# A fused attention and gated FFN kernel: the first batch's values computed token-major, the exchanged halves made by TensorE, the first FFN column finished first, later loads moved

**Chip, cores, metric.** One core of a Trainium2 chip. The metric is the device time of one execution in microseconds (us), smaller is better. An execution's time is about 1.7 us more than the span that its trace shows. "Order of time" means the list of an engine's instructions by their start; "the chain" is the chain of waits, followed back from the last instruction to what released each step.

## The reference, cut to what matters

```python
# q, k, v: (8 batches, 8 heads, 576 tokens, 64);  f: (8, 8, 576)
cum    = cumsum(log(clip(f, 1e-4, 1)))
scores = q @ k.T / 8 + cum[:, :, :, None] - cum[:, :, None, :]     # causal
x      = (softmax(scores) @ v) -> (4608 tokens, 512)
out    = (sigmoid(x @ w_gate) * (x @ w_val)) @ w_out               # d_ff = 1536
```

The decay of a key is folded into the values (`vg` = v times a factor per key), so the kernel computes exp(scores) and two sums: over values, and over the factors alone (the softmax's denominator).

## The kernel before

Batch 0 has nothing to run beside: its attention is a prologue. After it the FFN of one batch and the attention of the next share TensorE. Heads go in pairs (four per batch). A "column" is 128 of the 1536 FFN columns, gate and value; its product takes 16 matmuls over eight slots of `xR`, four with the heads in their own half of the partitions and four with the halves exchanged. The scores of a pair come in three units; their exp tiles are eA, eB and eC in the traces (for pair 2 of the changed kernel they lie in gv), and GpSimd lays the causal mask on each.

```python
def S_unit(p, u, slot, tag=None):          # scores of one unit, exp, causal mask
    ...
    nc.scalar.activation(e[...], ps[...], ACTF.Exp, scale=scale)
    nc.gpsimd.affine_select(out=m, in_=m, ...)

def out_one(p, bs, bv):                    # batch 0, one pair of heads
    pair_region(p, 512 * bs, 0, MAIN, False)      # ten matmuls with constant weights: sums
    nc.vector.transpose(Z, ps[:, bs, :])          # sums, reciprocal, spread again
    inverse(r, Z)
    spread(R, r)
    yield
    pair_region(p, 512 * bv, 0, MAIN, True)       # ten matmuls: values, features in partitions
    scaled(p, 512 * bv, R, 0, MAIN)               # xR = values * R
    if p == 0:
        cross_x(p, 1, 0, MAIN)                    # exchanged halves by two DMAs

def swap(p, bank):                         # exchanged halves by a matmul with a swap matrix
    nc.tensor.matmul(ps[:, bank, :], swap_bf, xR[:, p, 0:MAIN], start=True, stop=True)
    nc.scalar.copy(xR[:, HPAIR + p, 0:MAIN], ps[:, bank, :])

# ... the start of the program: loads
load_v(0, 0, 4, range(NJT), nc.sync)
load_qk(0, 0, ((0, 2), (2, 4)))            # GpSimd issues q and k
load_qk(0, 1, ((0, 4),))
load_v(0, 4, 8, range(NJT), nc.gpsimd)
load_w1(0, 512)
# ... the end of the prologue: columns 0 and 1 interleaved with the last pair's steps
swap(1, 0)
g1_slots(0, 0, (0, 1), True, False)        # column 0, slots 0 and 1
burst = out_one(HPAIR - 1, 2, 3)
next(burst)
g1_slots(0, 1, (0, 1), True, False)        # column 1, slots 0 and 1
swap(2, 1)
next(burst, None)
g1_slots(0, 0, (2, 5), False, False)
S_unit(0, "Z", 0, "D")
g1_slots(0, 1, (2, 5), False, False)
g1_slots(0, 0, (4, 6), False, False)
swap(3, 2)
g1_slots(0, 1, (4, 6, 3), False, False)
g1_slots(0, 0, (3, 7), False, True)
g1_end(0, 0)
g1_slots(0, 1, (7,), False, True)
g1_end(0, 1)
```

The softmax here doesn't subtract the row's maximum and nothing guards it: scores larger than these inputs give would overflow.

## Time and profile before

| | before |
|---|---|
| time, median of 3 (range) | 374.73 us (374.28 to 375.12) |
| first transposes of q and k | 6.72 us |
| first exponential | 8.93 us |
| last exponential of batch 0 starts | 21.6 us |
| first matmul of FFN column 2 | 29.37 us in the order of time, 29.87 in the chain |

The last row is the mark to follow: from there on TensorE is nearly always busy, so what the prologue gains or loses shows as a shift of that matmul. The two readings differ because of how column 2 starts: its first matmul began at 29.37, its second, into another PSUM bank, only at 29.87, and there the chain takes it up.

TensorE at the border, in the order of time (start, length, engine, line, operation, out<-in, form, count):

```profile
28.61 0.83 PE L195 MATMUL ps<-ident_bf,qk_in 64*64 64x64 bf16 x72
29.37 1.97 PE L455 MATMUL ps<-xR,w 64*128 64x512 bf16 x13
```

The 72 transposes end at 28.61 + 0.83 = 29.44, so the 0.70 us that the chain puts down to VectorE (29.12 to 29.82, in the prediction's lines) lie mostly beside transposes. Only column 2's second matmul waits for it.

### The profile page before, as it was taken

The numbers are of one execution on the slowest core, as the hardware profiler recorded it, in microseconds if no ns is written. First come the engines' busy times: TensorE is split into PE (matmuls) and PEld (weight loads), VectorE is DVE, ScalarE is ACT, GpSimd is POOL, SyncE is SP. The second block draws the span as 40 slices with busy tenths as digits, with TensorE's granted clock in tenths as the row PEclk, the third lists the DMA queues.
The fourth block names the chain that finished last, engine by engine and source line by source line (L and its number), as shares of the span: only waits on it lengthen the run. The fifth ranks groups of instructions, "written<-read, shape, count | busy, mean of one in ns | idle before, by whom it ended". The sixth has DMA issues, their size and how long they took to land.

```text
span 373.4 us, 12210 instructions
## 1 busy us (share of the span) xinstructions
PE 359.3 (96%) x5259; PEld 192.0 (51%) x5264; DVE 176.5 (47%) x382; ACT 195.7 (52%) x294; POOL 168.3 (45%) x265
## 2 busy tenths in 40 slices
PE   2889999999999999999999999999999999999996
PEld 1547545455555545454665566545456544444442
DVE  5775482557375555274708370737064703312320
ACT  5868754574736472848374727471747313323321
POOL 8896745064826663559665946460415000000000
PEclk9999999999999999999999999999999999999999
DMA  8999999599988976789984996596313131011002
GB/s 157 233 209 256 194 182 217 173 213 154 158 164 196 157 84 63 168 182 134 142 185 105 185 177 138 148 159 83 99 59 76 32 102 58 3 56 58 0 24 90
DMA packets 101350, 49.24 MB, mean 132 GB/s; under 512 B 72001, under 2 KB 94401, under 8 KB 101297
## 3 DMA queue, kind: packets, MB, share of 16 engines
q0 software_dynamic: 48704, 20.65, 44.0%
q1 hardware_dynamic: 52448, 27.68, 30.8%
q8 instruction: 41, 0.67, 0.8%
q10 hardware_dynamic: 144, 0.13, 0.1%
q14 instruction: 13, 0.10, 0.1%
HBM read 37.90 MB, written 9.44 MB: 127 GB/s over the span
## 4 chain that ended last, share of the span: by engine, by line
PE 94%; ACT 2%; DMA 1%; issue 1%; DVE 1%; POOL 0%; ACTq 0%; POOLq 0%
PE ps L455 51%; PE ps L495 17%; PE ps L352 8%; PE ps L504 8%; PE ps L241 6%; PE ps L195 2%; PE ps L300 1%; DMA qk_in<-in_k_dram 1%; ACT eC L246 1%; ACT eB L246 0%; ACT eA L246 0%; ACT kT L200 0%; PE ps L417 0%; DVE kT L200 0%; POOL qk_in L97 0%
## 5 line engine op out<-in xcount | busy, mean ns | idle before, releaser
L455 PE MATMUL ps<-xR,w 64*128 64x512 bf16 x1728 | 205.1, 376 | 0.2
L465 DVE SCALAR_TENSOR_TENSOR gv<-sg,ps 128x512 bf16<-128x512 bf16 x108 | 74.0, 686 | 152.2 <-ACT sg L464 149.0
L455 PEld LDWEIGHTS <-w 64*128 64x128 bf16 x1728 | 86.2, 94 | 84.0 <-issue 2.5
L464 ACT ACTIVATE sg<-ps 128x512 bf16<-128x512 f32 x108 | 64.5, 598 | 85.1 <-PE ps L455 83.9
L248 POOL TENSOR_SCALAR_AFFINE_SELECT eC<-eC 128x256 bf16<-128x256 bf16 x32 | 12.9, 404 | 94.4 <-ACT eC L246 94.4
L241 PE MATMUL ps<-qT,kT 64*128 64x320 bf16 (+6 forms) x416 | 47.0, 275 | 2.0 <-ACT kT L200 1.1
L246 ACT ACTIVATE eC<-ps 128x896 bf16<-128x896 f32 (+1 forms) x32 | 28.1, 878 | 20.7 <-PE ps L241 20.4
L257 POOL TENSOR_TENSOR vg<-vb,g_bf 128x640 bf16<-128x640 f32 x30 | 37.8, 1261 | 0.0
L482 ACT ACTIVATE ob<-ps 128x512 f32<-128x512 f32 x35 | 19.6, 596 | 32.2 <-PE ps L504 20.1
L495 PE MATMUL ps<-wox,gvx 64*128 64x512 bf16 x288 | 35.7, 376 | 0.0
L241 PEld LDWEIGHTS <-kT 64*128 64x128 bf16 x416 | 22.9, 96 | 24.0 <-issue 4.9
L246 ACT ACTIVATE eA<-ps 128x896 bf16<-128x896 f32 (+2 forms) x33 | 30.5, 926 | 9.0 <-PE ps L241 8.5
L495 PE MATMUL ps<-wo,gv 64*128 64x512 bf16 x288 | 34.4, 376 | 0.0
L246 ACT ACTIVATE eB<-ps 128x768 bf16<-128x768 f32 (+2 forms) x33 | 27.4, 832 | 10.0 <-PE ps L241 9.2
L504 PE MATMUL ps<-wo,gv 128*128 128x512 bf16 x140 | 32.1, 380 | 0.3 <-issue 0.2
L271 DVE TENSOR_TENSOR xR<-ps,R 128x64 bf16<-128x64 f32 (+2 forms) x68 | 26.2, 429 | 2.1
L108 POOL DMA_DIRECT2D vb<-in_v_dram x30 | 25.2, 849 | 0.2 <-issue 0.2
L263 DVE STREAM_TRANSPOSE R<-r 128x576 f32<-128x576 f32 (+1 forms) x32 | 24.6, 770 | 1.1
L495 PEld LDWEIGHTS <-gvx 64*128 64x128 bf16 x288 | 15.7, 94 | 13.0 <-issue 0.4
L495 PEld LDWEIGHTS <-gv 64*128 64x128 bf16 x288 | 15.3, 94 | 13.7 <-issue 0.5
L246 ACT ACTIVATE eD<-ps 128x640 bf16<-128x640 f32 x30 | 21.1, 702 | 2.0 <-PE ps L241 2.0
L504 PEld LDWEIGHTS <-gv 128*128 128x128 bf16 x144 | 13.4, 98 | 16.7 <-issue 1.4
(82 smaller groups left out, 325.9 us busy)
## 6 DMA issues: line engine op xcount, KB each, us to landing
out_dram<-ob SPq DMA_DIRECT2D x35, 256.0 KB, 2.2
vb<-in_v_dram POOLq DMA_DIRECT2D x20, 256.0 KB, 5.4
xR<-xR SPq DMA_DIRECT2D x20, 144.0 KB, 4.1
gvx<-gv SPq DMA_DIRECT2D x12, 192.0 KB, 4.8
vb<-in_v_dram SPq DMA_DIRECT2D x8, 256.0 KB, 7.3
k_rows<-in_k_dram POOLq DMA_DIRECT2D x16, 128.0 KB, 6.0
q_rows<-in_q_dram POOLq DMA_DIRECT2D x16, 128.0 KB, 5.6
qk_in<-in_q_dram POOLq DMA_DIRECT2D x7, 288.0 KB, 6.7
```

The lines of the kernel that those rows point to most:

```text
L108: eng.dma_start(vbs[b % 2][0:n, t, h0:h1, :], rows)
L241: nc.tensor.matmul(ps[:, sc + h, c:c + i1 - i0], k_at(p, jt)[hp, :], qT[hp, i0:i1], start=True, stop=True)
L246: nc.scalar.activation(e[:, :, 0:w], ps[:, sc:sc + 2, 0:w], ACTF.Exp, scale=scale)
L257: (eng or nc.gpsimd).tensor_tensor(out=vg[:, :, :, 0:D], in0=vbs[b % 2][:, :, 2 * a:2 * a + 2, :], in1=g_bf[:, :, 2 * p:2 * p + 2].unsquee ...
L263: nc.vector.transpose(R.rearrange("p (n c) -> p n c", c=32), r.unsqueeze(2).to_broadcast([128, r.shape[1], 32]))
L271: nc.vector.tensor_tensor(out=xR[:, a, r0:r0 + n], in0=psf[:, o + i:o + i + n], in1=R[:, i:i + n], op=ALU.mult)
L352: nc.tensor.matmul(psf[32 * qd:32 * qd + 32, o + a:o + z], lhsT_of(jt, qd), e_of(u, qd)[:, c:c + z - a], start=(y == 0), stop=(y == len(to ...
L455: nc.tensor.matmul(ps[:, bk, :], w1[half, head, ft * NP:(ft + 1) * NP], xR[half, sl, t0:t0 + TCH], start=(first and x == 0), stop=(last an ...
L464: nc.scalar.activation(sg, ps[:, fb, :], ACTF.Tanh, scale=0.5)
L465: nc.vector.scalar_tensor_tensor(out=gv[:, ft, :], in0=sg, scalar=1.0, in1=ps[:, fb + 1, :], op0=ALU.add, op1=ALU.mult)
L495: nc.tensor.matmul(ps[:, bk, :], lhsT, rhs, start=(x == 0 and ft == 0), stop=(x == 1 and ft == NFT - 1))
L504: nc.tensor.matmul(ps[:, 4 + tt, :], gv[:, ft, tt * NP:(tt + 1) * NP], wo[:, ft, :], start=(ft == 0), stop=(ft == NFT - 1))
```

## The change

Its intent: spare the prologue work. Values are computed with tokens in the partitions (the exp tile is the stationary operand, `vg` with one more column the moving one), so the 65th column of each product is the sum and the constant-weight matmuls fall away. The normalised result is turned back by TensorE transposes, in both orders of the halves, so that pairs 1 to 3 need no swap matmul and no DMA. Values are loaded pair by pair and mostly after q and k. Column 0 is finished before column 1 starts. The output weights and the q/k of later batches load at later steps.

```diff
+    def vals_main(p, bank, todo):            # 40 matmuls of 65 columns for a pair
+        ...
+    def norm_main(p, bank):                  # reciprocal of column 65, product, into gv
+        ...
+    def back(p, its, swapped, at):           # turn back, own or exchanged halves
+        ...
-    load_v(0, 0, 4, range(NJT), nc.sync)
     load_qk(0, 0, ((0, 2), (2, 4)))
...
-    load_v(0, 4, 8, range(NJT), nc.gpsimd)
-    load_w1(0, 512)
...
+    load_v(0, 0, H, (NJT - 1,), nc.sync)
+    load_v_pair(0, 0)
+    load_qk(0, 1, ((0, 4),))
+    load_v_pair(0, 1)
...
     T_step(0, 4, ACTC, DVEC)
+    nc.scalar.activation(gT, cum, ACTF.Exp, ...)     # was before T_step
+    load_v(0, 4, 8, range(NJT - 1), nc.gpsimd)
+    S_unit(0, "U", 0)
...                                            # in the loop over pairs
+        if p == 0:
+            load_w1(0, 512)
+        main_unit(p, 2)                        # the scores, exp and mask of unit eC
...                                            # the end of the prologue
+    vals_main(3, 0, EARLY3)
+    norm_main(3, 0)
+    back(2, range(4), 0, main_at)
+    back(2, range(4), 1, lambda it: 2048 + NP * it)
+    nc.scalar.copy(xR[:, HPAIR + 2, 0:MAIN], psh[:, 2048:2048 + MAIN])
+    vals_main(3, 1, LATE3)
+    norm_main(3, 1)
+    nc.vector.tensor_copy(split(xR[:, 2, 0:MAIN]), main_of)
     g1_slots(0, 0, (0, 1), True, False)
...
+    for swapped, copy in ((0, nc.vector.tensor_copy), (1, nc.scalar.copy)):
+        o = 3072 + MAIN * swapped              # both halves in PSUM bank 3
+        back(3, range(4), swapped, lambda it: o + NP * it)
+        copy(xR[:, HPAIR * swapped + 3, 0:MAIN], psh[:, o:o + MAIN])
+    g1_slots(0, 0, (2, 5, 4, 6), False, False)
...
     g1_slots(0, 0, (3, 7), False, True)
     g1_end(0, 0)
+    S_unit(0, "Z", 0, "D")
+    g1_slots(0, 1, (0, 1, 2, 5, 4, 6, 3, 7), True, True)
     g1_end(0, 1)
...
-    for x, w in enumerate((5, 9, 12)):         # steps at which wo loads
+    for x, w in enumerate((5, 19, 20)):
-    for x, w in enumerate((18, 21, 22, 23)):   # steps at which later q/k load
+    for x, w in enumerate((21, 23, 50, 54)):
```

## The prediction

> **What bounds the kernel now.** I read the page first, then busy time by stretch, then the chain of waits over the first 64 us, then the order in time of GpSimd, VectorE and TensorE there, and last the DMA traffic of the first 9 us.
>
> The page gives the frame: engine totals, then TensorE by slices of 9.3 us.
>
> ```profile
> span 373.4 us, 12210 instructions
> PE 359.3 (96%) x5259; PEld 192.0 (51%) x5264; DVE 176.5 (47%) x382; ACT 195.7 (52%) x294; POOL 168.3 (45%) x265
> PE   2889999999999999999999999999999999999996
> ```
>
> TensorE is idle 14.1 us in all, and almost only in the first slices and in the last. The stretches say it in us (columns: stretch, length, busy time and count of PE, weight load, DVE, ACT, POOL, then clock, DMA share, GB/s):
>
> ```profile
> 0.00:17.08 17.08, 9.36 (x168) 5.71 (x172) 10.86 (x29) 11.03 (x14) 15.16 (x31) 1.00 1.00 194
> 17.08:28.61 11.53, 10.44 (x153) 5.48 (x154) 7.86 (x14) 7.64 (x12) 10.53 (x17) 1.00 1.23 209
> 28.61:62.00 33.39, 32.89 (x583) 18.45 (x582) 16.36 (x33) 24.39 (x38) 21.84 (x38) 1.00 1.15 211
> ```
>
> The change rewrites the prologue, all that comes before the repeating FFN steps. That border is at 28.61 us, where the 72 transposes of the next batch start. After it TensorE loses 0.5 us in 33, and its work there is not changed. So the time moves by about as much as the first matmul of FFN column 2 moves. In the chain that matmul starts at 29.87, 0.75 us after TensorE was free, because VectorE has not emptied column 0's banks:
>
> ```profile
> 28.68 0.43 PE ps L195 x36
> 29.11 0.01 issue
> 29.12 0.70 DVE gv L465
> 29.82 0.04 issue
> 29.87 2.77 PE ps L455 x23
> ```
>
> The start of the prologue hangs on loads. In the window 3 to 9 us the queue of q and k (q0) has to share with that of v (q1), and carried 0.66 MB in 6 us, 110 KB/us; alone it later runs at about 200 GB/s:
>
> ```profile
> q0 software_dynamic: 633, 0.66, 65.1%
> q1 hardware_dynamic: 2314, 0.57, 47.3%
> ```
>
> In the chain the first k piece is awaited until 6.68 (2.07 + 4.61). From 8.93 to 22.19 the exponentials and copies keep ScalarE busy for about 11.5 of 13.3 us.
>
> **What the Trainium skill says.** "TensorE: Matmul & The Clock Gate", Part 1: the array starts at half clock and is released after some 3.4 us of sustained work, judged in free-running windows. The trace agrees in effect: 36 transposes take 0.69 to 0.80 us up to 13 us and 0.50 at 17.00. The clock row does not show it. The same page, in its part on the 56 ns gap, puts the floor of start-to-start at about 25 ns; here 39 matmuls of 65 columns on half-width tiles stand in the chain with 0.81 us, 21 ns each, so I use the trace. "Trainium Kernel Development and Optimization", Key Constraints: the queues share the same 16 DMA engines; the two q lines above agree. "TensorEngine Tiling", PSUM Bottleneck: faster TensorE packing does not speed up emptying PSUM. That is the crux below.
>
> **The change, part by part.**
>
> *Removed on TensorE:* per pair of heads, the ten matmuls with the constant weights that make sums already spread over 64 rows (1.27 us cold at 13.29, 0.7 warm), the ten value matmuls (1.21 and 0.7), and the swap matmuls (3 x 0.39). *Added:* 40 value matmuls of 65 columns per pair, whose last column is the sum: 0.81 us warm, 1.25 cold (estimate from 0.81 and the half clock, as they are partly bound by issue); and 8 transposes back per pair (16 for pairs 1 to 3, own and swapped half): half of 16 x 128 columns at the rate of 512 columns in 0.21 us is 0.45 warm. So 2.5 cold becomes about 2.1, and 1.7 warm becomes about 1.3: 1 to 1.5 us less TensorE work, where TensorE waits anyway for much of the time.
>
> *VectorE:* per pair it loses a transpose of the sums (0.72), a spreading transpose (0.71) and keeps a reciprocal (0.25) and a product (0.69); it gains a copy back (0.65 for 512 columns, from 0.76 for 576) and, for pairs 2 and 3, the scaled values that GpSimd made in 1.26 (0.95 each on VectorE with its small copy). Four pairs: 9.5 + 1.9 = 11.4 before, (0.24 + 0.71 + 0.65 + 0.95) x 4 = 10.2 after. Hardly less, and in a chain.
>
> *Loads:* v comes by pair, after q and k, so q and k have the engines nearly alone from about 4.6 us. 288 KB then land at about 5.95 instead of 6.68: 0.75 us gained at the head.
>
> Now the chain, in the order of the new program's queues, with the durations of the old one. First transposes 5.95; copies 6.7 to 7.45; first scores 7.5; the exp of the decays now stands after the copy on ScalarE (7.35 to 8.1), so the first exp starts at 8.15 (before 8.93) and the exps of pair 1 at 11.75 (before 12.10).
>
> Then GpSimd. Its ten issues after the identity (v pair, q, k, v pair, four v) at 0.75 or 0.63 each run from 4.45 to 11.7. Masks of eA and eB follow to 12.75; then two issues of FFN weights (0.7 each) stand **before** the mask of eC, which ends at about 14.55 (before: 13.88). The values of pair 0 need it, and stand in TensorE's queue ahead of the scores of pair 2. So they end at about 15.5, scores of pair 2 at 16.15, its exp starts at 16.2 (before 16.75). Of the 0.75 gained, 0.55 is left.
>
> From 15.55 VectorE is the chain: normalise pair 0 (0.95) 16.5; values of pair 1 scaled 17.4; copy 18.1; q copy 18.85; normalise pair 1, after its values, 19.8; scaled 20.7; copy 21.35; scaled 22.25; normalise pair 2 at 23.15; first half of pair 3 23.8. TensorE then turns pair 2 back (0.5) and makes the late half of pair 3 (0.6): 24.3. Normalise 24.95; copy pair 2 25.6; copy pair 3 26.3. The product of column 0 with the slots that need them (12 matmuls, 107 ns each) ends at 26.95, the small Z scores at 27.15. All 16 of column 1 (1.73) come after: 28.9. Two sets of transposes: 29.3.
>
> There column 2 can start at once, as column 0's banks were emptied from 27.0 to 28.3. So 29.35 against 29.87: **0.5 us gained**: 0.75 from the bank wait that is gone, less 0.2 because the prologue itself ends no earlier. Moving the output weights and q/k loads changes no wait that I find: in the chain, wo is not awaited, and its loads now issue at about 47.5 us with the queue empty, some 10 us before use. I take 0.2 more for less crowding in the queue, and round to 373.9 from 374.73.
>
> **Rivals.**
> (a) *GpSimd or VectorE is quicker than I say.* The old first mask took 0.95 where its kind takes 0.40, next to a VectorE product; with less collision the chain starts 0.5 earlier, and shorter VectorE operations give 1 us more: 372.5. For it: the new form spares TensorE and GpSimd (two products of 1.26). Against: VectorE got that work.
> (b) *Late clock.* TensorE stands still for about 1.2 us at 13.3 to 14.5, before the values of pair 0. If the window that released the clock at 17.0 is thereby not full, the release comes one 3.4 us window later. I reckon 0.3 to 0.5 us, as VectorE paces that stretch: 374.3; more if TensorE turns out to pace it: 375.
> (c) *Loads of later stages shift the wait.* FFN weights 0 to 511 issue at 12.75 and land near 20, before column 0 at 24.3; but if the software queue is slower, column 0 waits. Or the later issues of wo and of q/k of batch 3 come too late: wo's last third issues at step 20 and is needed at step 32, q/k of batch 3 have 13 steps. Old landings take 2.5 us for 512 KB plus 1.7 to start. Unlikely; would cost 1 to 2 us: 375.5.
> (d) *Column-first order costs.* Column 1's 16 products cannot fill waits for pair 3 any more. In the old program they did; this is in my sum (1.73 after column 0), and is what eats most of the gain. If pair 3 is ready sooner than 26.3, it is a gain of up to 1.5.
>
> **Range and chances.** The border can move only inside the prologue: TensorE is busy 19.8 us of it (9.36 + 10.44), loses at most 1.5 of that, and cannot begin before about 6, so the border would stay past 24 even without idle time; a gain of 2% (7.5 us) needs it at 21. I give it 0.02, for what I cannot see. A loss of 7.5 us needs a new wait in every later stage: 0.01. (a) and (d) together reach 372.3, (b) and (c) 375.3; that is my range, near 8 in 10.
>
> **What would show it.** Right: first transposes of k near 6.0; first exp near 8.15; values of pair 0 held by the mask of eC until about 14.5; VectorE without gaps from 16 to 24; no wait on VectorE before column 2, which starts near 29.3. Wrong: column 2 before 28 (VectorE was not the chain) or after 30.5 (late clock or a load); any wait over 0.5 us on wo, FFN weights or q/k after 30 us.

## More of the kernel before

The waits of TensorE in the first 30 us of the kernel before (columns: who <- for whom: us in total, times, longest):

```profile
PE ps L195 <- DMA qk_in<-in_q_dram: 5.5, 1, 5.5
PE ps L241 <- ACT kT L200: 1.1, 1, 1.1
PE ps L195 <- DMA qk_in<-in_k_dram: 1.0, 1, 1.0
PE ps L300 <- DVE Z L319: 0.5, 1, 0.5
```

Only the first is long, and it is the first load.

At the end of the prologue the products of columns 0 and 1 (L455) stand between the other steps, and from the values of pair 3 on the chain names no wait (start, us, what):

```profile
24.67 0.74 PE ps L300 x10
25.41 0.54 PE ps L455 x4
25.95 0.15 PE ps L241 x10
26.09 0.86 PE ps L455 x8
26.95 0.32 PE ps L332
27.28 1.40 PE ps L455 x12
```

## The result, and the profile after

| | before | after |
|---|---|---|
| time, median of 4 (range) | 374.50 us (373.98 to 375.12) | 376.93 us (376.42 to 377.68) |
| span of the profiled execution | 373.4 | 374.7 |
| first transposes | 6.72 | 6.19 |
| first exponential | 8.93 | 8.40 |
| last exponential of batch 0 starts | 21.6 | 21.6 |
| column 2 in the order of time (in the chain) | 29.37 (29.87) | 30.64 (30.71) |
| second pair of matmuls of column 2 | 29.87 | 30.87 |
| first transposes to column 2, in the order of time | 22.65 | 24.45 |
| of it TensorE idle, in gaps over 60 ns | 2.34 | 4.58 |

The ratio of the times is 1.0066, with a 95% interval of 1.0042 to 1.0089: slower, by less than 2%. (Ratios here are the mean time of one kernel's fast runs over that of the other's of the same rounds, so not quite the ratio of the medians that I quote.) The predicted time was 373.9 and the range ended at 375.3, so the result is outside.

Taken as a sum, the rest of the kernel is level: from column 2 to the end, the trace of before has 373.4 - 29.37 = 344.03 us and that of after 374.7 - 30.64 = 344.06. So the net difference of the two traces, 1.3 us, is that of the prologue. In its parts the rest is not the same: after stops for 1.28 us at 109.13 (told below), and TensorE of before is busy 0.9 us less in 80 to 100, 120 to 140 and 240 to 260 us (19.76, 19.57 and 19.70 us, against 19.94, 20.00 and 20.00). The profiled execution of before was the slowest of its runs and that of after the quickest of its, which is why the medians differ by 2.4.

The page of after, to set against the first lines in the prediction:

```profile
span 374.7 us, 12464 instructions
PE 358.2 (96%) x5393; PEld 192.2 (51%) x5397; DVE 174.2 (46%) x384; ACT 195.4 (52%) x295; POOL 168.5 (45%) x262
```

TensorE's busy time fell by 1.1 us and yet the span rose by 1.3. So it waits more. Its waits in the first 31 us of after:

```profile
PE ps L202 <- DMA qk_in<-in_q_dram: 5.0, 1, 5.0
PE ps L202 <- DMA qk_in<-in_k_dram: 2.1, 2, 1.2
PE ps L248 <- DVE kT L207: 0.9, 1, 0.9
PE ps L248 <- DVE vg L265: 0.7, 1, 0.7
PE ps L375 <- DVE xR L664: 0.6, 1, 0.6
```

The first is shorter by half a microsecond: the head start. The second holds, with its longest of 1.2 us, k of heads 4 to 7, for which before did not wait. The third is the first scores waiting for the copied keys; before, the decay's transposes filled that stretch, and now they come after it. The last is new: TensorE waits for a copy by VectorE. The chain of waits of after, in two parts (start, us, what; pieces of "issue" under 0.05 us left out):

```profile
6.60 7.05 DMA qk_in<-in_k_dram
13.70 0.69 PE ps L202 x18
14.39 0.33 PE ps L248 x2
14.71 1.43 PE ps L347 x40
16.14 0.56 PE ps L248 x2
16.72 1.94 ACT gv L255 x2
...
20.17 1.32 POOL w L159 x2
21.49 1.09 POOL eA L257
22.58 0.61 POOL eB L257
23.23 0.32 PE ps L347 x8
...
25.79 0.43 DVE xR L664
26.27 0.41 PE ps L375 x8
26.68 1.40 PE ps L507 x12
28.08 0.14 PE ps L248 x10
28.23 1.73 PE ps L507 x16
29.95 0.76 PE ps L202 x72
30.71 1.83 PE ps L507 x16
```

The first part says that the second half of k, issued at 6.60, landed only 7.05 us later, and that the third set of transposes waited for it. In before it took about as long (7.3 us) but was issued at 5.23: what moved it is that the first values now stand ahead of it in GpSimd's queue. By 16.72, when the exponentials of pair 2 start, the head start is gone (16.75 before). Between the parts the chain runs over GpSimd: two issues of FFN weights and the masks of pair 3. The second part is the end: VectorE copies pair 3, only then do eight transposes make its exchanged half, only then 12 matmuls finish column 0, and column 1's 16 follow in one piece. Nothing is left to run beside those steps.

Where the 1.27 us between the two columns 2 arise can be read off the last exponential, which starts at 21.59 in before and at 21.65 in after: up to there 0.06 us are lost (the head start is gone), and 1.21 after it. That stretch repeats. It takes 7.78, 7.79, 7.78 and 8.12 us in before, `before_lateloads`, `before_warm` and `before_keep`, and 8.99, 9.15, 8.86, 8.85, 8.99 and 8.63 in after, `after_again`, `after_oldloads`, `after_warm`, `after_head` and `after_both`, which leave the end as the change has it. In all ten traces the full clock had been granted before that stretch began, so the clock does not make this part of the difference.

GpSimd at the two places where it holds masks back (in brackets: idle before, and what ended it):

```profile
13.94 0.69 POOL L159 DMA_DIRECT2D w<-in_moe_w_val_dram  x1 [0.43 <-DMA qk_in<-in_k_dram]
14.63 0.42 POOL L257 TENSOR_SCALAR_AFFINE_SELECT eC<-eC 128x256 bf16<-128x256 bf16 x1
...
21.48 1.09 POOL L257 TENSOR_SCALAR_AFFINE_SELECT eA<-eA 128x256 bf16<-128x256 bf16 x1
```

The issue at 13.94 waited for the landing of the k load that uses the same semaphore: GpSimd's loads signal on eight semaphores in turn (numbers 99 to 106 in the trace), so the ninth load waits until the first has landed. The mask at 21.48 took 1.09 us instead of about 0.40, beside a VectorE product of two operands in SBUF from 21.50 to 22.32. "GPSIMD Engine Reference", Specifications, of the Trainium skill names contention of GpSimd with such VectorE instructions; the trace agrees.

### The profile page after: what moved, and what is told of

Read it like the earlier page. It is cut to its first block, busy times and chain, and to the rows that moved or that the text cites. A ratio compares the mean times of both kernels' runs of the same rounds, so it can differ in the third digit from the quotient of the medians.

```text
span 374.7 us, 12464 instructions
## 1 busy us (share of the span) xinstructions
PE 358.2 (96%) x5393; PEld 192.2 (51%) x5397; DVE 174.2 (46%) x384; ACT 195.4 (52%) x295; POOL 168.5 (45%) x262
## 3 DMA queue, kind: packets, MB, share of 16 engines
q0 software_dynamic: 48864, 21.11, 45.8%
## 4 chain that ended last, share of the span: by engine, by line
PE 90%; ACT 2%; POOL 2%; DMA 2%; DVE 1%; issue 1%; POOLq 0%; ACTq 0%; DVEq 0%
PE ps L507 49%; PE ps L547 17%; PE ps L556 8%; PE ps L404 8%; PE ps L248 5%; DMA qk_in<-in_k_dram 2%; PE ps L202 2%; POOL qk_in L98 1%; ACT gv L255 1%; PE ps L347 1%; ACT eC L255 0%; PE ps L375 0%; POOL vb L114 0%; POOL w L159 0%; POOL eA L257 0%
## 5 line engine op out<-in xcount | busy, mean ns | idle before, releaser
L248 PE MATMUL ps<-qT,kT 64*128 64x320 bf16 (+6 forms) x416 | 47.9, 275 | 2.1 <-DVE kT L207 0.9
L255 ACT ACTIVATE eC<-ps 128x896 bf16<-128x896 f32 (+1 forms) x31 | 27.5, 886 | 20.5 <-PE ps L248 20.5
L266 POOL TENSOR_TENSOR vg<-vb,g_bf 128x640 bf16<-128x640 f32 x28 | 35.3, 1262 | 0.2 <-issue 0.2
L255 ACT ACTIVATE eA<-ps 128x896 bf16<-128x896 f32 (+2 forms) x32 | 29.4, 923 | 7.2 <-PE ps L248 6.7
L255 ACT ACTIVATE eB<-ps 128x768 bf16<-128x768 f32 (+2 forms) x32 | 26.4, 827 | 9.9 <-PE ps L248 9.2
L280 DVE TENSOR_TENSOR xR<-ps,R 128x64 bf16<-128x64 f32 (+2 forms) x64 | 23.5, 412 | 1.7
L547 PEld LDWEIGHTS <-gvx 64*128 64x128 bf16 x288 | 15.8, 94 | 12.7
L272 DVE STREAM_TRANSPOSE R<-r 128x576 f32<-128x576 f32 x28 | 21.8, 778 | 1.0
L556 PEld LDWEIGHTS <-gv 128*128 128x128 bf16 x144 | 13.4, 98 | 16.7 <-issue 1.4
```

The lines of the kernel that those rows point to most:

```text
L248: nc.tensor.matmul(ps[:, sc + h, c:c + i1 - i0], k_at(p, jt)[hp, :], qT[hp, i0:i1], start=True, stop=True)
L255: nc.scalar.activation(e[:, :, 0:w], ps[:, sc:sc + 2, 0:w], ACTF.Exp, scale=scale)
L266: (eng or nc.gpsimd).tensor_tensor(out=vg[:, :, :, 0:D], in0=vbs[b % 2][:, :, 2 * a:2 * a + 2, :], in1=g_bf[:, :, 2 * p:2 * p + 2].unsquee ...
L272: nc.vector.transpose(R.rearrange("p (n c) -> p n c", c=32), r.unsqueeze(2).to_broadcast([128, r.shape[1], 32]))
L280: nc.vector.tensor_tensor(out=xR[:, a, r0:r0 + n], in0=psf[:, o + i:o + i + n], in1=R[:, i:i + n], op=ALU.mult)
L547: nc.tensor.matmul(ps[:, bk, :], lhsT, rhs, start=(x == 0 and ft == 0), stop=(x == 1 and ft == NFT - 1))
```

## The experiments

My theory after reading the traces had three parts: (1) the head start is lost to q/k of heads 4 to 7 and the masks behind GpSimd's issues; (2) the end of the prologue lost its filler; (3) the later loads do nothing. Rivals: the clock of TensorE is released later and that is all of it; or the moved loads are.

**The change again, and the load places alone, both ways.** `after_again` is the changed kernel, unchanged. `after_oldloads` puts the places back, `before_lateloads` puts them into the kernel before:

```diff
-    for x, w in enumerate((5, 9, 12)):
+    for x, w in enumerate((5, 19, 20)):
-    for x, w in enumerate((18, 21, 22, 23)):
+    for x, w in enumerate((21, 23, 50, 54)):
```

> The changed kernel once more, as it is. Theory A: its trace shows TensorE standing still for 1.28 us near 109 us (no wait named), and that comes from the later q/k loads crowding the DMA engines, so it comes back at the same place within 2 us, and the time is again about 2.4 us over the kernel before. Rival B: that stop is an accident of one execution; then this trace has no such stop there (or has one elsewhere), and the first matmul of FFN column 2 is late by more than the 0.84 us that the first pair of traces shows.

> Only the load places put back (output weights at steps 5, 9, 12; q/k of batches 2 and 3 at 18, 21, 22, 23). Theory A: the stop near 109 us is gone, column 2 still starts near 30.7, the time falls by about 1.3 us (ratio to the changed kernel 0.9966). Rival B: no stop to remove, time within 0.4 us of the changed kernel.

> The kernel before with the new load places alone. Theory A: a stop of about 1.3 us near 108 us appears and the time rises by 1 to 1.5 us over the kernel before. Rival B: within 0.4 us of the kernel before.

Measured, beside 374.80 us for the kernel before: `after_again` 376.25, ratio 1.0043 (1.0021 to 1.0065), with column 2 at 30.70 and the stop at 109.12 again (1.09 us); `after_oldloads` 377.51, 1.0073 (1.0050 to 1.0096); `before_lateloads` 375.02, 0.9999 (0.9975 to 1.0023). The slowness repeats, and the load places neither make it nor heal it. They do move one thing: in many executions TensorE stops for about 1 us with no wait named. With the late places it is at 108 to 110 us, with the old ones at 48 to 50 (1.22 us at 49.91 in `after_oldloads`). It is not always there: the traces of before, `after_warm` and `after_head` have none over 0.6 us. The two late ones, in the order of time, first of after, then of `before_lateloads`:

```profile
109.13 0.22 PE L202 MATMUL ps<-ident_bf,qk_in 64*64 64x64 bf16 x3 [1.28 <-issue]
```

```profile
108.47 1.68 PE L495 MATMUL ps<-wox,gvx 64*128 64x512 bf16 x13 [1.01 <-issue]
```

In `before_lateloads` the queue that carries instructions moved two packets, 0.03 MB in all, between 100 and 112 us. That the stop is a wait for them is likely but was not tested. Moving it gained nothing.

**The filler at the end.** `after_fill` puts four matmuls of column 1 between the two turnings of pair 3:

```diff
         o = 3072 + MAIN * swapped
+        if swapped:
+            g1_slots(0, 1, (0, 1), True, False)
         back(3, range(4), swapped, lambda it: o + NP * it)
...
-    g1_slots(0, 1, (0, 1, 2, 5, 4, 6, 3, 7), True, True)
+    g1_slots(0, 1, (2, 5, 4, 6, 3, 7), False, True)
```

> The changed kernel, with the four products of column 1 that need pairs 0 and 1 alone put between the two turnings of pair 3, where TensorE waits 0.59 us for VectorE's copy out of the same PSUM bank. Theory A (prologue waits are what makes column 2 late): the wait is filled, column 2 starts 0.4 to 0.55 us sooner, the time falls by the same. Rival: VectorE's copy gets later or the wait moves to the turning of pair 2's columns in the banks of column 1, and less than 0.2 us is gained.

Measured: 376.09 us, ratio 1.0032 (1.0008 to 1.0057); column 2 at 29.84 in the order of time, against 30.64 in after. The same steps, in the order of time, of after and then of `after_fill`:

```profile
25.11 0.57 PE L375 MATMUL ps<-ident_bf,gv 128*64 128x128 bf16 x8
26.27 0.41 PE L375 MATMUL ps<-ident_bf,gv 128*64 128x128 bf16 x8 [0.59 <-DVE xR L664]
```

```profile
24.55 0.57 PE L375 MATMUL ps<-ident_bf,gv 128*64 128x128 bf16 x8
25.14 0.61 PE L507 MATMUL ps<-xR,w 64*128 64x512 bf16 x4
25.71 0.41 PE L375 MATMUL ps<-ident_bf,gv 128*64 128x128 bf16 x8
```

The wait of 0.59 us is gone, filled with work that had to be done anyway. But of the 0.80 only 0.26 arose here: the last exponential had already started 0.54 sooner (21.11), in an execution whose clock was released at 16.83 us and not at 18.34, and from there to column 2 it took 8.73 us instead of 8.99. In the times it is hardly to be seen beside `after_again` of the same chip.

**The end rebuilt.** `after_tail` spreads the matmuls of columns 0 and 1 over the last pair's steps and puts the exchanged half of pair 3 into another PSUM bank:

```diff
+    g1_slots(0, 0, (0, 1), True, False)
     vals_main(3, 0, EARLY3)
...
+    g1_slots(0, 0, (5,), False, False)
     vals_main(3, 1, LATE3)
...
-        o = 3072 + MAIN * swapped
+        o = 0 if swapped else 3072
...
-    g1_slots(0, 0, (2, 5, 4, 6), False, False)
+    g1_slots(0, 1, (0, 1, 5, 4), True, False)
+    g1_slots(0, 0, (2, 6), False, False)
```

> The changed kernel, with the products of columns 0 and 1 put between the steps of pair 3 again (those of pairs 0 and 1 as soon as their inputs are there), and pair 3's second turning in another PSUM bank. Theory (ii): from the last exponential to column 2 it takes about 7.9 us instead of 9.0, column 2 starts near 29.6, the time falls by about 1 us. Rival (VectorE's chain of normalising and copies sets column 2): still 8.7 us or more, time within 0.4 us.

Measured: 375.86 us beside 374.37, ratio 1.0036 (1.0001 to 1.0072). From the start of the last exponential to column 2 it took 8.5 us; after took 9.0, before 7.8. The second turning no longer waits for VectorE's copy, so it was the shared bank that tied them. 0.5 us are won in this trace, 0.7 are still missing.

What holds the rest was not tested. One thing stands in the traces: the change gives the product that scales the values of pair 3 to VectorE, and one of the three masks of pair 3 then takes 0.82 to 1.29 us (0.98 in `after_tail`) in every version in which that product ran beside them. In before and its five variants the three take 0.40 to 0.41, 0.63 to 0.64 and 0.40 to 0.41, and in `after_spv` and `after_best`, where the product waited for its loads, at most 0.44, 0.64 and 0.41. No run moves this product back. It cannot be all: in `after_again` the chain does not run over these masks, and the stretch is no shorter (9.15).

**Column first in the kernel before.** `before_colfirst` takes only the order of the columns:

```diff
-    g1_slots(0, 1, (0, 1), True, False)
...
-    g1_slots(0, 1, (2, 5), False, False)
...
-    g1_slots(0, 1, (4, 6, 3), False, False)
...
-    g1_slots(0, 1, (7,), False, True)
+    g1_slots(0, 1, (0, 1, 2, 5, 4, 6, 3, 7), True, True)
```

> The kernel before, with nothing but the product of FFN column 0 finished ahead of that of column 1. Theory E (column-first gives up the filler that the products of column 1 were for pair 3's chain): column 2 starts later than 29.4, by 0.5 to 1 us, the bank wait of 0.43 us being taken off already; the time rises by as much. My prediction's own view: the bank wait that is gone is worth as much as what is lost, column 2 within 0.3 us of 29.4.

> Column 0's product first, now with the clock released early in both, against before_keep. Theory E (column 1's products were filler for pair 3's chain): column 2 starts 0.5 to 1 us later than in before_keep. My prediction's view: within 0.3 us. In before_colfirst the clock came at 22.9 us by accident, which hid this.

`before_colfirst`: 375.11 us beside 374.31, ratio 1.0013 (0.9998 to 1.0027). Its profiled execution had the full clock only from 22.89 us, so its column 2 (33.43) says little; from the last exponential to there it took 8.3 us, 0.5 more than before. `before_colfirst_keep` adds the two spare matmuls told below: 374.11 beside 374.22, 0.9996 (0.9978 to 1.0014), and 8.9 us for that stretch, against 8.1 in `before_keep`. So the order lengthens the end by 0.5 to 0.8 us in both traces. The times do not show it; their intervals allow up to 1.0 and 0.5 us. Alone it is not the 1.6 to 2.5 us.

**The clock.** Spare matmuls at the start (11 of 512 columns, and 2 after the first transposes) release it early:

```diff
+    nc.vector.memset(wo[:, 0, :], 0.0)
+    warm(11)
...
     T_step(0, 4, ACTC, DVEC)
+    warm(2)
```

> The kernel before, with 11 matmuls of 512 columns on a zeroed tile ahead of the first transposes and 2 after them, into a bank that nobody reads; TensorE would else stand idle there. Theory F (the array's half clock, released at 17.1 to 18.7 us in the traces so far, costs in the prologue): the clock is released by about 7 to 8.5 us, column 2 starts 0.5 to 1 us sooner, the time falls by 0.2 to 0.4%. Rival (ScalarE and VectorE pace that stretch): release as early, but column 2 within 0.3 us.

> The changed kernel with the same 13 idle-time matmuls. Theory F: the changed kernel, released later (18.3 to 18.7 in three of four traces), gains more than the kernel before does, 1 to 1.5 us, and the gap between the two kernels shrinks to under 0.8 us. Rival (the chain of waits on VectorE, GpSimd and the loads makes it late): it gains no more than the kernel before, and stays 1.2 us or more behind before_warm.

Measured, beside 374.31: `before_warm` 375.79, ratio 1.0040 (1.0022 to 1.0059); `after_warm` 375.76, 1.0048 (1.0022 to 1.0074). The stretches of `after_warm`, cut at its clock events (times of the clock are those of the trace's clock records; ahead of the first record the view prints 1.00, and I take it as half, since 36 transposes take 0.69 to 0.80 us before the release and 0.50 after it; stretch, length, busy time and count of PE, weight load, DVE, ACT, POOL, then clock, DMA share, GB/s):

```profile
2.21:5.62 3.41, 3.41 (x10) 1.09 (x8) 2.14 (x9) 1.68 (x2) 3.33 (x7) 1.00 1.07 176
5.62:9.03 3.41, 2.82 (x89) 1.54 (x87) 1.56 (x4) 2.90 (x6) 3.41 (x6) 1.00 0.99 188
9.03:12.44 3.41, 1.31 (x32) 0.58 (x20) 2.03 (x4) 3.41 (x5) 3.41 (x6) 1.00 1.16 249
12.44:15.86 3.42, 2.65 (x78) 2.04 (x80) 0.89 (x2) 1.50 (x3) 3.42 (x8) 0.50 0.86 180
15.86:19.27 3.41, 3.34 (x92) 2.39 (x90) 2.69 (x6) 2.97 (x4) 2.25 (x5) 0.50 1.24 205
```

The clock is full from 5.62, the window with 2.82 us of work keeps it, the one with 1.31 loses it at 12.44, and only the window with 3.34 brings it back at 19.27. Time at half clock between the first transposes and column 2 fell from 12.15 us (after) to 6.83, and yet the stretch took 24.47 us, against 24.45. One execution each, and the early full clock fell into the stretch in which TensorE waits for loads. So it says that an early release alone does not mend after; it does not say that the half clock from 12.44 on costs nothing, and `after_keep` below says that it does. In the kernel before it is worth something: the same stretch took 21.84 us in `before_warm` (7.30 to 29.14) and 22.65 in before, but there the spare matmuls delayed the first transposes.

Keeping the clock with few spare matmuls at the places where TensorE idles:

```diff
+        if p == 0:
+            warm(2)              # ahead of the scores of pair 1 (in before: p == 1, at the loop's top)
...
+            if p == 1:
+                warm(3)          # ahead of the third transposes; after_keep only
```

> The kernel before with two spare matmuls of 512 columns (real data, into a bank that nobody reads) in the one gap of TensorE over 0.3 us between 7 and 19 us, ahead of the scores of pair 1 (idle 0.92 to 1.05 us there). Theory F2: the clock is released at the end of the first free-running window of 3.41 us in which TensorE hardly stood still; the gap then decides when. Now TensorE is without gaps from about 6.7 us, so the release comes between 10.1 and 13.6 us, 3.5 us sooner than in the first trace, column 2 starts about 1 to 1.5 us sooner, and the time falls by 1 to 2 us (ratio 0.995 to 0.997). Rival (ScalarE and VectorE pace the prologue): release as early, column 2 within 0.3 us, same time.

> The changed kernel with two such matmuls ahead of the scores of pair 1 and three ahead of the third transposes, where it stands 0.7 and 0.7 to 1.2 us. Theory F2: release between 11 and 14.5 us instead of 18.3 to 18.7, column 2 near 29.3 (30.65 without), time 1 to 1.5 us less. If the late clock is all that makes the changed kernel slower, it ends level with before_keep; if the chain of waits is the other half, it stays about 0.8 us behind.

`before_keep`: 374.21 beside 374.22, ratio 1.0003 (0.9983 to 1.0023). In its traced execution the spare matmuls did not do what they were for: the clock was released at 17.15, not between 10.1 and 13.6, and column 2 came at 30.83. A miss; with the same two matmuls `before_colfirst_keep` had the full clock from 12.12. `after_keep`: 375.93, 1.0044 (1.0020 to 1.0068); the clock was full from 12.72, the last exponential started at 20.5, 1.1 us before that of after, and still column 2 came at 31.31, as the clock was withdrawn from 22.96 to 26.37 after a window with 1.95 us of work:

```profile
19.55:22.96 3.41, 1.95 (x68) 1.53 (x63) 2.94 (x8) 2.01 (x4) 3.41 (x6) 1.00 1.20 217
22.96:26.37 3.41, 3.37 (x56) 2.32 (x56) 1.09 (x4) 0.58 (x1) 3.41 (x6) 0.50 1.24 207
```

No gain in the times, so this is no remedy. It does show what the clock is worth in the head: from the first transposes to the last exponential it took 14.48 us in `after_keep`, 15.46 in after. At a like clock the kernel before is still quicker there: 13.75 in `before_colfirst_keep`, and 14.87 in before itself.

**The loads and masks at the head.** `after_both` issues q/k of heads 4 to 7 ahead of the values, and the first FFN weights after the mask of eC:

```diff
-    load_v_pair(0, 0)
     load_qk(0, 1, ((0, 4),))
+    load_v_pair(0, 0)
...
-        if p == 0:
-            load_w1(0, 512)
         main_unit(p, 2)
+        if p == 0:
+            load_w1(0, 512)
```

> The changed kernel with q and k of heads 4 to 7 loaded ahead of v of pair 0 (undoes the wait of the third transposes), and the first FFN weights issued after the mask of eC instead of before it. Theory D (TensorE's stop before the third transposes, 0.7 to 1.2 us at 12 to 13.7 us, starts the lateness): the stop falls under 0.2 us, the values of pair 0 end about 1 us sooner, column 2 starts 0.5 to 1.2 us sooner (near 29.7). Rival (the mask of eC on GpSimd holds the values of pair 0 anyway; VectorE is the chain after that): under 0.3 us.

Measured: 377.50 beside 374.31, ratio 1.0083 (1.0064 to 1.0102). The wait of the third transposes was gone, but GpSimd's later issues now stood against the landing of those very loads, and the masks behind them moved back (first mask in after: done at 12.2), and column 2 came at 30.96. GpSimd, order of time:

```profile
10.83 0.75 POOL L109 DMA_DIRECT2D vb<-in_v_dram  x1 [0.66 <-DMA qk_in<-in_q_dram]
12.52 0.75 POOL L109 DMA_DIRECT2D vb<-in_v_dram  x1 [0.94 <-DMA qk_in<-in_k_dram]
13.27 0.68 POOL L257 TENSOR_SCALAR_AFFINE_SELECT eA<-eA 128x256 bf16<-128x256 bf16 x1
```

`after_tuned` combined the earlier q/k with `warm(2)` and `warm(1)` at the two places above and the other bank for pair 3:

> The changed kernel mended at three places: q and k of heads 4 to 7 ahead of v, spare matmuls in its gaps (2 and 1), and pair 3's second turning in a bank that VectorE doesn't read. Waits before the third transposes and of 0.59 us before the second turning should be gone; column 2 near 28.5, time at or under that of the kernel before, 1.5 us under the changed kernel or more. Rival: VectorE and GpSimd hold it, column 2 not under 29.3.

Measured: 377.15 beside 374.22, ratio 1.0091 (1.0068 to 1.0115). The same wait, now 1.75 us for the landing of k, and TensorE waited 1.49 us for the mask of eC. Both are misses of mine: an order of issues was changed without counting the loads to the eighth.

So I took four issues away from GpSimd. `after_spv` issues q/k of heads 4 to 7 early and gives the values of heads 4 to 7 to SyncE, held back by a tiny write on VectorE; `after_best` is the same with the rebuilt end:

```diff
-    load_v(0, 4, 8, range(NJT - 1), nc.gpsimd)
...
         if p == 0:
+            nc.vector.memset(vbs[0][:, 0:NJT - 1, 4:8, 0:1], 0.0)
+            load_v(0, 4, 8, range(NJT - 1), nc.sync)
             load_w1(0, 512)
```

> The changed kernel with v of heads 4 to 7 issued by SyncE after the second transposes (four issues less on GpSimd, 3 us), and q and k of heads 4 to 7 ahead of v of pair 0. Theory (i): masks of pair 0 end near 11 and 13 us instead of 12.8 and 15.1, the third transposes start near 12 without a stop, the exps of pair 2 start near 15 instead of 16.7 and the last one near 20 instead of 21.6; column 2 1 to 1.5 us sooner, time 1 to 1.5 us less. Rival (the half clock or VectorE paces that stretch): the exps of pair 2 not before 16.2.

> Both. If the two add up, column 2 near 28.3 and the time 2 to 2.5 us under the changed kernel, at or a little under the kernel before (ratio 0.997 to 1.001). If one hides the other: no better than the better of the two.

Measured, beside 374.37: 384.60, ratio 1.0248 (1.0211 to 1.0285), and 382.57, 1.0201 (1.0164 to 1.0238). The masks of pair 0 ended at 9.7, 11.1 and 12.8 us, the exponentials of pair 2 started at 15.8 and the last one at 20.9, as hoped. But the scaled values of pair 2 waited, the clock was withdrawn meanwhile (24.59 to 38.24), and column 2 came at 40.11. VectorE in `after_spv`, order of time:

```profile
25.94 0.83 DVE L266 TENSOR_TENSOR vg<-vb,g_bf 128x640 bf16<-128x640 f32 x1 [6.25 <-DMA vb<-in_v_dram]
```

The four loads were issued between 10.85 and 12.42 us and landed at 15.24, 18.92, 22.29 and 25.82, beside 1 MB of FFN weights and the next batch's q and k. Two more runs asked whether such loads are slow by themselves or by company:

```diff
# after_spv_early: issued after the first copies, at about 7.5 us (with the rebuilt end)
     T_step(0, 4, ACTC, DVEC)
     nc.scalar.activation(gT, cum, ACTF.Exp, ...)
-    load_v(0, 4, 8, range(NJT - 1), nc.gpsimd)
+    nc.vector.memset(vbs[0][:, 0:NJT - 1, 4:8, 0:1], 0.0)
+    load_v(0, 4, 8, range(NJT - 1), nc.sync)
# after_spv_w1late: as after_best, weights after the mask of eC, next q/k at pair 2
```

> As after_best (v of heads 4 to 7 issued by SyncE after a tiny write that waits for VectorE, q/k of heads 4 to 7 issued ahead of v of pair 0, tail with filler), but the first FFN weights are issued after the mask of eC and the next batch's q/k at pair 2, so that v of heads 4 to 7 has the DMA engines to itself. In after_best the last of these four loads landed some 14 us after its issue, beside 2 MB of weights and q/k, and the scaled values of pair 2 waited for it by 6 us. Theory (that wait is contention for the DMA engines by later-needed loads): the v loads land by about 17 to 18 us, no wait over 1 us for them, exps end near 21, column 2 starts at 28.5 to 29.5, time 372.5 to 374.5. Rival (the many small rows of that load are slow by themselves on that queue): they still land after 20 us, column 2 after 32, time over 376.

> As after_best, but v of heads 4 to 7 is issued by SyncE at about 7.5 us, some 3 us earlier, beside q/k of heads 4 to 7, with the weights where the changed kernel has them. Theory (contention with weights): the v loads are mostly down before the weights start, land by about 15 to 17 us, q/k of heads 4 to 7 land up to 1.5 us later than in after_best; last exp 21 to 21.6, column 2 at 28.8 to 30, time 373 to 375.5. Rival (slow by themselves): the last lands some 14 us after its issue again, 21 to 22 us, column 2 after 31, over 376.

Measured, beside 373.96: `after_spv_w1late` 377.69, ratio 1.0093 (1.0053 to 1.0132); `after_spv_early` 375.22, 1.0031 (0.9993 to 1.0068). Issued at 7.30, 7.76, 8.90 and 9.47 us the same loads landed at 13.99, 14.94, 15.48 and 16.79, in 6.6 to 7.3 us, where the last of `after_spv` took 13.4: it is company. In `after_spv_w1late` they landed at 15.53, 15.86, 17.64 and 21.06: the weights went out at 11.68 all the same, as GpSimd was free by then, and the q/k that I had moved to pair 2 stood, with the next weights, ahead of pair 3's masks: GpSimd issued from 19.58 to 22.15, and the first of these masks came only then. The theory's numbers failed; of the rival's, the last landing (21.06) and the time came true and column 2 (30.98) did not, but as the loads again had company this does not show them slow by themselves.

`after_spv_early` has the quickest prologue of all changed versions: last exponential at 20.8, column 2 at 29.45, level with before. Its profiled execution was the quickest of its four, though. Hence the last run, the head alone with the end as the change has it:

> The load repair of after_spv_early alone (q/k of heads 4 to 7 ahead of v of pair 0 in GpSimd's queue, v of heads 4 to 7 by SyncE at about 7.5 us), with the tail as the changed kernel has it. Theory (head and tail lose time one after the other, about 0.7 us each): last exp near 20.9 instead of 21.6, from there to column 2 the 9.0 us of the changed kernel, so column 2 at 29.8 to 30.1, time about 0.5 us under the changed kernel: 375 to 376.3, ratio 1.002 to 1.005. Rival (the head start is lost in the tail anyway, as in after_keep, where the last exp came at 20.5 and column 2 at 31.3): column 2 at 30.5 or later, ratio 1.005 to 1.007.

Measured: 375.31 beside 374.94, ratio 1.0012 (0.9985 to 1.0038), better than expected. Its trace is no witness for that: the profiled execution (376.13 us) had the full clock only from 20.13, its last exponential at 22.3 and column 2 at 31.26. From the last exponential to column 2 it has the 9.0 us of after. By the times alone the head would be the larger of the two causes, but the intervals of `after_head`, `after_tail` and `after_spv_early` overlap, and the traces say the opposite: 1.21 of the 1.27 us between before and after come after the last exponential has started. No version beats the kernel before.

## Why the prediction was wrong

Its steps against the trace of after (us; the last three rows from the chain):

| step as predicted | predicted | measured | late by |
|---|---|---|---|
| first transposes | 5.95 | 6.19 | 0.24 |
| first exp | 8.15 | 8.40 | 0.25 |
| exps of pair 1 | 11.75 | 11.84 | 0.09 |
| mask of eC done | 14.55 | 15.05 | 0.50 |
| exp of pair 2 | 16.2 | 16.72 | 0.52 |
| VectorE's last copy (pair 3) done | 26.3 | 26.22 | -0.08 |
| column 0 done | 26.95 | 28.08 | 1.13 |
| column 1 done | 28.9 | 29.95 | 1.05 |
| column 2 starts | 29.35 | 30.71 | 1.36 |

- **The head.** The first load did come earlier, by 0.53 instead of 0.75 us. The half microsecond to the exp of pair 2 was lost where the prediction had allowed only for the mask: q/k of heads 4 to 7 landed at 13.65, and GpSimd's weight issue waited 0.43 for the same landing. The landing time of these loads was a step that the prediction did not work out at all; it only counted the issues.
- **VectorE's chain.** Its end was right, by two errors that cancel: it began 0.6 us late (16.18, not 15.55), and copies of 128x512 took 0.42 us where I had put 0.65.
- **The step that failed.** "The product of column 0 with the slots that need them (12 matmuls, 107 ns each) ends at 26.95." The 12 matmuls took 1.40 us, near enough; but they started at 26.68, not at about 25.7. The exchanged half of pair 3 is turned only after VectorE's copy of the own half, because both lie in one PSUM bank: 0.59 us of wait and 0.41 of transposes stand ahead of the product. `after_fill` and `after_tail` take this wait away, and from the last exponential to column 2 it then takes 8.7 and 8.5 us instead of 9.0. So what the prediction had wrong is the path: it let TensorE run the 12 products beside VectorE's last copies, while the program puts the second turning, which hangs on one of these copies, ahead of all 12.
- **"Two sets of transposes"** were put at 0.4 us; the 72 took 0.76, as they had in before (28.61 to 29.37): I had taken the 36 that the chain names for all. With the 1.05 above that is the 1.36.
- **"0.75 from the bank wait that is gone"** was some 0.3, as shown above: the chain's line was read as idle time without looking at what TensorE did beside it.
- **TensorE's saving**, put at 1 to 1.5 us, was 0.44 in the prologue: (22.65 - 2.34) before against (24.45 - 4.58) after.
- **A reading of the page on TensorE.** The part on the 56 ns gap of "TensorE: Matmul & The Clock Gate" puts the floor of start-to-start at about 25 ns, and I set 21 ns against it. That was no contradiction: the 40 matmuls of 65 columns at 21.57 us of after start in pairs, one for each half of the columns of the stationary operand, and from pair to pair it is 32 ns.
- **The rivals.** (b), the late clock: it was indeed released later, at 18.34 against 17.08, and a still earlier release quickens the head (`after_keep`), but the end, where 1.21 us are lost, ran at full clock in both. (c), later loads: no effect. (d), column first costs: right in kind, and I had counted it in the sum; what I missed is that it also leaves the second turning bare. My sign "after 30.5" came true, but the cause that I had set beside it, late clock or a load, is at most that of the head.
- **Open.** The traces carry 0.8 us (chain), 1.0 (second pair of column 2) or 1.3 us (order of time); the times say 1.6 to 2.5. The rest lies in executions that left no trace. When the clock is released varied from 16.83 to 22.89 us between executions without early spare matmuls, which may be the spread, but I have not shown that it takes after harder than before. In the two traces the end is the larger part; that repairing it brings the time down is not shown, as `after_tail` lies within the noise of `after_again`.

## What to carry to other kernels

Work that waits for nothing is worth more in the places where an engine would idle than as a tidy block: before putting one product first, list what filled the gaps. When loads are reordered, work out their landings and the semaphores that later issues have to get back, not only the issues. And read a wait in the chain against the order of time of the waiting engine, before booking it as gain.

## What the Trainium skill lacked or had wrong

- "TensorE: Matmul & The Clock Gate", Part 1, puts the return to half clock after an idle window. Here it came back after windows that were far from idle: 1.31 of 3.41 us busy (`after_warm`) and 1.95 (`after_keep`); windows with 2.82 and, in `after_keep`, 2.62 kept it. It was not released by a window with 2.65 us of work, but by those with 3.34 and 3.37. Busy time alone does not decide it: in `before_keep` no release followed a window with 3.24 (10.32 to 13.74), and one followed the next, with 3.08.
- No page that I found has it: in these programs a load issued by GpSimd waits until the load eight places before it, which signals on the same semaphore, has landed. It cost 0.43 us in after, 0.66 and 0.94 in `after_both`, 1.75 in `after_tuned`.
- "Runtime: NRT & Kernel Launch", Instruction fetch mechanics, gives no duration for a fetch that comes late. If the stops of TensorE with no wait named are such fetches (likely, not tested), they take about 1 us: 1.28 at 109.13 us in after, 1.01 at 108.47 in `before_lateloads`, 1.22 at 49.91 with the old load places.
